# Attention and a gated MLP on one core: the attention of two batches as one stream of nine tiles

## The chip, the cores and the metric

The kernel runs on one core of one Trainium2 chip. The metric is the time of one execution on the device in microseconds; the time before is the median of three runs. The trace comes from a further, profiled execution. Engines are named as the profile names them: PE is TensorE (PEld its weight loads), DVE VectorE, ACT ScalarE, POOL GpSimd, SP SyncE, whose queue issues the transfers.

## The reference

Eight batches of 8 heads, 576 tokens and 64 elements a head go through attention in chunks of 64 tokens, then through an MLP whose gate mixes the tokens of a batch:

```python
scores = scale * np.matmul(q_c, k_c.transpose(0, 1, 2, 4, 3))      # per chunk of 64 tokens
attn = np.exp(scores - np.max(scores, axis=-1, keepdims=True))
attn = attn / (np.sum(attn, axis=-1, keepdims=True) + 1e-09)
x = heads_side_by_side(np.matmul(attn, v_c))                       # 8 x 576 x 512
h = gelu_tanh(x @ w_in)                                            # 512 -> 1024
u, v = (h[..., :512], h[..., 512:])
v_n = (v - mean(v)) / np.sqrt(var(v) + 1e-06) * g_ln
v_s = np.einsum('ts,bsd->btd', w_sg, v_n) + b_sg[None, :, None]    # over the 576 tokens
return x + (u * v_s) @ w_out
```

The inputs are spread so that one float32 rounding does not do: the kernel splits each operand of a large product into a high and a low part and adds three products.

## The kernel before

**Tiles of attention.** The 8 x 576 tokens are 36 tiles of 128 tokens, counted through all batches. 576 is four and a half tiles, so the tiles that begin in a batch of even number are five (the fifth lies half in the next batch), in one of odd number four: batch 2 has tiles 9 to 13, batch 3 tiles 14 to 17. `last` and `first` (lines 257 and 258) hold the bounds. From tile 5 on, a tile goes through three steps. S, the scores (`att_scores`, L315: 16 matmuls on 64x64 quadrants, 32 records in the trace, into a half of the tile `banks`), with the softmax behind it: maximum (L324), addition (L338) and sum (L342) on DVE, the exponential on ACT (L341), the scaling by the reciprocal sum on POOL (L345). T, the transposition (`att_transpose`: DVE in blocks of 32 at L359, ACT and DVE copies into `ptT` at L362 to L369). O, the outputs (`att_out`, L397: 16 small matmuls a tile, a pair of tiles into one accumulator `pm`), and `keep`, which copies them out as `xf`, as high part `xh` (ACT, L93) and low part `xl` (DVE, L96). S and O take one tile or a pair.

**Units of the MLP.** A batch has v units (12 matmuls of 128x512, L439; five in an even batch, of which the last, m = 4, takes the first 64 tokens of this batch and of the next from `xodd`; four in an odd one), four u units (L476), four s units (the mixing of tokens, 28 matmuls of 128x288, L496) and four o units (24, L519). I write v0 to v4, u0 to u3, s0 to s3, o0 to o3. Behind v and u stands a Gelu on ACT (L442, L483), and behind v the normalisation: DVE (L445 to L447), a power on POOL (L448), high part on ACT (L456) and low part on DVE (L457). Behind s the product with u on DVE (`gt`, L500), its high part on ACT (`gh`) and its low part on DVE (`gl`); every o unit needs `gh` and `gl` of all four s units, those of s3 in its last quarter. Behind o the residual addition on DVE (L527) and the store on SP. Exponential and Gelu stand in different tables of ACT; where one follows the other, the program has an ACT_TABLE_LOAD.

**Buffers.** Accumulators `pm` come from a ring of three in PSUM (`ps_m`, L89), for units and outputs alike. `xh`, `xl`, `gh` and `gl` of a batch share a ring of four places (tag `big`, L409, L410, L505, L506). The tiles q, k, v have four places (`QKV_BUFS`); `scores` issues the loads up to two tiles beyond its own (L540).

**Order.** The opening is written out in `START` (L45), up to the o units of batch 0 and the u units of batch 1. Then for every batch b from 1 on the units run in the order v, u, s, o, and `att_slots` (L543) hangs the steps of the next batch's attention behind units by their number: `"10:T0"` is the transposition of that batch's tile 0 behind unit 10. `SLOTS` (L56) has one list for a next batch of four tiles (b even, 17 units) and one for five (b odd, 16 units). Within this, a scheduler may still move instructions where their operands are expected to be ready. Each engine then works through its instructions in order.

Of the kernel before, what the change touches and what calls it, by code (L numbers as in the profile page):

```python
# [11 lines left out]
F32R = mybir.dt.float32r  # L12
# [9 lines left out]
B, H, S, D = 8, 8, 576, 64  # L22
P = 128
# [3 lines left out]
NT = B * S // P  # L27
HP = H // 2
KT = DM // P
# [14 lines left out]

START = """  # L45
L0 A0 A1 L1 S0 L2 T0 D11 A2 W0 A3 W1 L3 A4 S1 W2 S2 w0 w1 W3 T1 O0 w2 S3 O1 T2 w3 D14 A5 O2 T3 S4 O3 M0 X0 T4 X1 v00
O4 x0 v01 x1 X2 v02 X3 x2 v03 x3 v04 Y0 u00 u01 G0 Y1 u02 P5 u03 T5 s00 T6 s01 Q5 P7 Y2 s02 T7 Y3 s03 T8 v10 Q7 v11 Y4 v12 Y5 v13 u10 Y6 u11 Y7 u12 u13 o00 o01 o02 o03
"""

PE_TILES = 5  # L50
# [2 lines left out]

SLOTS = {  # L56
    4: "8:S01 10:T0 11:T1 12:O01 12:S23 14:T2 15:T3 16:O23",
    5: "7:S01 8:T0 9:T1 10:O01 10:S23 11:S4 12:T2 13:T3 14:T4 15:O23 15:O4",
}


# [6 lines left out]
def segments(t):  # L68

    out, at, end = [], t * P, (t + 1) * P  # L70
    while at < end:
        b = at // S
        stop = min(end, (b + 1) * S)
        out.append((b, at - t * P, at - b * S, stop - at))
        at = stop
    return out
# [3 lines left out]
def block_attention_gated_mlp(ctx: ExitStack, tc: tile.TileContext, qkv, w_in, w_out, w_sg, g_ln, b_sg, out):  # L80
# [3 lines left out]
    xp = ctx.enter_context(tc.tile_pool(name="xp", bufs=2))  # L84
# [6 lines left out]
    def split(hi, lo, src, hi_eng, lo_eng):  # L91
        if hi_eng is nc.scalar:
            nc.scalar.copy(hi, src)  # L93
        else:
            hi_eng.tensor_copy(hi, src)
        lo_eng.tensor_tensor(lo, src, hi.bitcast(F32), op=ALU.subtract)  # L96
# [160 lines left out]
    last = [((b + 1) * S - 1) // P for b in range(B)]  # L257
    first = [0] + [last[b] + 1 for b in range(B - 1)]
    xf, xh, xl, xodd = {}, {}, {}, {}
# [112 lines left out]
    def att_out(*tiles):  # L372
# [29 lines left out]
        for t, xo in zip(tiles, xos):  # L402
            keep(t, xo)

    def keep(t, xo):
        for b, at, off, n in segments(t):
            if b not in xf:
                xf[b] = xp.tile([P, HP, S], F32, name="xf")
                xh[b] = xp.tile([P, HP, S], F32R, name="xh", tag="big", bufs=4)  # L409
                xl[b] = xp.tile([P, HP, S], F32R, name="xl", tag="big", bufs=4)  # L410
            cs = slice(at // D, (at + n) // D)
            src = xo[:, cs]
            dst = [a[b][:, :, off : off + n].rearrange("p hp (c s) -> p c hp s", s=D) for a in (xh, xl, xf)]
            if f"l{t}" in ON_POOL:
                nc.scalar.copy(dst[2], src)
                split(dst[0], dst[1], dst[2], nc.scalar, nc.gpsimd)
            else:
                split(dst[0], dst[1], src, nc.scalar, nc.vector)
                nc.scalar.copy(dst[2], src)  # L419
            if off == 0:  # L420
                if b % 2 == 0:
                    xodd[0] = [xp.tile([P, HP, 2 * ODD], F32R, name=f"xodd_{i}", bufs=1) for i in range(2)]
                c = slice(b % 2 * ODD, (b % 2 + 1) * ODD)
                for dst, src in zip(xodd[0], (xh[b], xl[b])):
                    nc.scalar.copy(dst[:, :, c], src[:, :, 0:ODD].bitcast(F32))
# [59 lines left out]
    gh, gl = {}, {}  # L485

    def s_unit(b, dt):
        pm = ps_m.tile([P, 2, 512], F32, name="pm")
        dc = slice(dt * P, (dt + 1) * P)
        ops = []  # L490
        for m in range(4):
            ops += [(vl[m], wsg_h, m), (vh[m], wsg_l, m), (vh[m], wsg_h, m)]
        ops += [(z2[b % 2], wsg_l, 4), (z1[b % 2], wsg_h, 4)]
        for i, (a, c, m) in enumerate(ops):
            for j in range(2):
                nc.tensor.matmul(  # L496
                    pm[:, j, :HS], a[:, dc], c[:, m, j * HS : (j + 1) * HS], start=(i == 0), stop=(i == len(ops) - 1)
                )
        gt = tmp.tile([P, S], F32, name="gt", tag="tmp")
        nc.vector.tensor_tensor(  # L500
            gt.rearrange("p (a c) -> p a c", a=2), pm[:, :, :HS],
            u2[0][:, dt, :].rearrange("p (a c) -> p a c", a=2), op=ALU.mult,
        )
        if dt == 0:
            gh[b] = xp.tile([P, KT, S], F32R, name="gh", tag="big", bufs=4)  # L505
            gl[b] = xp.tile([P, KT, S], F32R, name="gl", tag="big", bufs=4)  # L506
        split(gh[b][:, dt, :S], gl[b][:, dt, :S], gt, nc.scalar, nc.vector)

    def o_unit(b, et):
# [33 lines left out]
    def att_slots(b, n):  # L543

        slots = [[] for _ in range(n)]
        for step in SLOTS[last[b] + 1 - first[b]].split():
            i, what = step.split(":")
            f = {"S": scores, "T": att_transpose, "O": att_out}[what[0]]
            slots[int(i)].append((f, [first[b] + int(k) for k in what[1:]]))
        return slots  # L550

    steps = {
# [3 lines left out]
    for name, f in zip("vuso", (v_unit, u_unit, s_unit, o_unit)):  # L556
        steps[name] = (lambda f: lambda k: f(k // 10, k % 10))(f)
# [12 lines left out]
    for b in range(1, B):  # L570
        units = [(v_unit, m) for m in range(4 if b % 2 else 5)]
        units += [(u_unit, i) for i in range(4)]
        units += [(s_unit, i) for i in range(4)] + [(o_unit, i) for i in range(4)]
        slots = att_slots(b + 1, len(units)) if b + 1 < B else [[]] * len(units)
        for i, ((f, k), after) in enumerate(zip(units, slots)):
            if b > 1 or f in (s_unit, o_unit):
                f(b, k)
            for g, tiles in after:
                g(*tiles)
# [44 lines left out]
```

## Time and profile before

| | |
|---|---|
| median of 3 runs | 532.47 us (530.79 to 532.74) |
| profiled execution | 531.17 us, span 529.4 us |
| PE matmuls / weight loads | 504.3 us (95%) / 465.8 us (88%) |
| DVE, ACT, POOL | 350.3 us (66%), 261.8 us (49%), 79.7 us (15%) |
| TensorE clock granted | 0.996 of full speed |
| data moved | 46.57 MB, 88 GB/s on average |

A row of a timeline gives the start in us, the time to the end of the last instruction of the group, engine, line, operation, output and inputs, sizes and number of records; brackets name idle time of the engine before it and who ended it. Matmuls overlap, so the distance from start to start is their price, not the duration shown.

### The profile page before, as it was taken

How to read it: one execution, taken by the hardware profiler on the slowest of the kernel's cores; microseconds unless marked ns; L12 is line 12 of the kernel's file. 1: busy time of each engine (PE TensorE's matmuls, PEld its weight loads, DVE VectorE, ACT ScalarE, POOL GpSimd, SP SyncE). 2: the span in 40 equal slices, each digit the busy share in tenths (PEclk: the TensorE clock that was granted, in tenths of full speed). 3: DMA queues.
4: the chain of work that ended last, by engine and by line, in shares of the span. 5: the costliest groups of instructions: out<-in, count | busy, mean ns of one | idle time of the engine just before them, and what ended most of it. 6: DMA issues, size and time to landing. Idle time of an engine off the chain costs nothing.

```text
span 529.4 us, 12456 instructions
## 1 busy us (share of the span) xinstructions
PE 504.3 (95%) x5274; PEld 465.8 (88%) x5278; DVE 350.3 (66%) x718; ACT 261.8 (49%) x482; POOL 79.7 (15%) x80
## 2 busy tenths in 40 slices
PE   5989996989999999999999999999999999999996
PEld 4677896779989799999989799998999799998996
DVE  7989677797587556766387555767378564767042
ACT  4697665654163753554353753544363653545210
POOL 0122221210102121012002121012012021012000
PEclk9999998999999999999999999999999999999999
DMA  8832524113441700352032700352033700020002
GB/s 336 286 117 61 164 68 121 42 41 110 140 122 68 202 1 1 106 165 61 2 109 80 198 5 1 83 173 75 2 79 106 199 7 1 3 90 0 1 1 89
DMA packets 49594, 46.57 MB, mean 88 GB/s; under 512 B 35202, under 2 KB 39554, under 8 KB 49540
## 3 DMA queue, kind: packets, MB, share of 16 engines
q1 hardware_dynamic: 49540, 45.80, 28.8%
q8 instruction: 41, 0.67, 0.5%
q14 instruction: 13, 0.11, 0.1%
HBM read 36.34 MB, written 9.44 MB: 86 GB/s over the span
## 4 chain that ended last, share of the span: by engine, by line
PE 75%; DVE 11%; ACT 6%; DMA 3%; POOL 2%; issue 1%; SPq 0%; DVEq 0%; POOLq 0%
PE pm L519 19%; PE pm L496 19%; PE pm L476 17%; PE pm L439 15%; PE pm L397 3%; PE banks L315 2%; DMA wsg<-w_in 1%; DMA qkv_t<-qkv 1%; DVE xl L96 1%; POOL pt L345 1%; DVE den L342 1%; DVE gt L500 1%; DMA st<-w_out 1%; DVE pt L338 1%; ACT xf L419 1%
## 5 line engine op out<-in xcount | busy, mean ns | idle before, releaser
L496 PE MATMUL pm<-wsg,v 128*128 128x288 f32 x768 | 108.7, 297 | 0.0
L496 PEld LDWEIGHTS pm<-wsg,v 128*128 128x128 f32 x768 | 104.0, 189 | 0.7
L519 PE MATMUL pm<-gh,wout 128*128 128x288 f32 x512 | 91.2, 297 | 0.0
L519 PEld LDWEIGHTS pm<-gh,wout 128*128 128x128 f32 x512 | 75.8, 189 | 0.4
L345 POOL TENSOR_TENSOR pt<-pt,den 128x512 f32<-128x512 f32 x32 | 35.1, 1104 | 239.6 <-DVE den L344 119.2
L448 POOL TENSOR_TENSOR sm<-sm,neg_half 128x1 f32<-128x1 f32 x36 | 35.1, 976 | 152.6 <-DVE sm L447 149.9
L519 PE MATMUL pm<-gl,wout 128*128 128x288 f32 x256 | 55.6, 296 | 0.0
L476 PE MATMUL pm<-xh,win_l 128*128 128x288 f32 x256 | 55.1, 297 | 0.0
L476 PE MATMUL pm<-xh,win_h 128*128 128x288 f32 x256 | 55.0, 296 | 0.0
L476 PE MATMUL pm<-xl,win_h 128*128 128x288 f32 x256 | 55.0, 296 | 0.0
L439 PE MATMUL pm<-win_h,xl 128*128 128x512 f32 x128 | 51.9, 406 | 2.4 <-DVE xl L96 2.4
L439 PE MATMUL pm<-win_l,xh 128*128 128x512 f32 x128 | 51.0, 399 | 0.0
L439 PE MATMUL pm<-win_h,xh 128*128 128x512 f32 x128 | 50.7, 396 | 0.0
L324 DVE TENSOR_REDUCE nmax<-banks 128x8 f32<-128x512 f32 x31 | 21.2, 684 | 39.7 <-PE banks L315 39.6
L93 ACT CAST gh<-gt 128x576 fp32r<-128x576 f32 x32 | 21.6, 674 | 44.6 <-DVE gt L500 44.2
L476 PEld LDWEIGHTS pm<-xh,win_l 128*128 128x128 f32 x256 | 41.4, 188 | 0.8
L519 PEld LDWEIGHTS pm<-gl,wout 128*128 128x128 f32 x256 | 41.4, 189 | 0.0
L476 PEld LDWEIGHTS pm<-xh,win_h 128*128 128x128 f32 x256 | 41.1, 188 | 0.0
L476 PEld LDWEIGHTS pm<-xl,win_h 128*128 128x128 f32 x256 | 41.0, 189 | 0.0
L362 ACT COPY ptT<-blocks 128x512 f32<-128x512 f32 x31 | 19.2, 621 | 43.1 <-DVE blocks L359 31.3
L500 DVE TENSOR_TENSOR gt<-pm,u 128x576 f32<-128x576 f32 x32 | 24.1, 752 | 24.0 <-PE pm L496 23.8
L341 ACT ACTIVATE pt<-pt 128x512 f32<-128x512 f32 x34 | 21.5, 632 | 36.5 <-DVE pt L338 26.6
(125 smaller groups left out, 842.5 us busy)
## 6 DMA issues: line engine op xcount, KB each, us to landing
qkv_t<-qkv SPq DMA_DIRECT2D x32, 512.0 KB, 4.6
out_dram<-ot SPq DMA_DIRECT2D x31, 288.0 KB, 2.2
qkv_t<-qkv SPq DMA_DIRECT2D x124, 64.0 KB, 3.8
qkv_t<-qkv SPq DMA_DIRECT2D x3, 768.0 KB, 10.0
wsg<-w_in SPq DMA_DIRECT2D x4, 512.0 KB, 4.5
wout<-w_in SPq DMA_DIRECT2D x4, 512.0 KB, 8.1
st<-w_out SPq DMA_DIRECT2D x8, 256.0 KB, 2.7
stage<-w_sg SPq DMA_DIRECT2D x5, 288.0 KB, 2.8
```

Source lines behind the costliest of these rows:

```text
L93: nc.scalar.copy(hi, src)
L324: nc.vector.tensor_reduce(nmax if t < PE_TILES else nmax.rearrange("p (c hp) -> p c hp", c=2), sc, axis=AX.X, op=ALU.max, negate=True)
L341: nc.scalar.activation(pt, pt, AF.Exp, scale=scale)
L345: (nc.gpsimd if t > last[1] else pick(f"n{t}")).tensor_tensor(pt, pt, den.unsqueeze(2).broadcast_to([P, H, D]), op=ALU.mult)
L362: nc.scalar.copy(ptT, blocks)
L397: nc.tensor.matmul(xo[o, c, h // 2, :], qt[r, 2, place, :], ptT[r, place].rearrange("p a s -> p (a s)"), start=True, stop=True,)
L439: nc.tensor.matmul(pv, a[:, kt, tok], c[:, kt, DH:], start=(i == 0), stop=(i == 11))
L448: nc.gpsimd.tensor_tensor(rs, rs, neg_half, op=ALU.pow)
L476: nc.tensor.matmul(pm[:, j, :HS], a[:, kt, dc], c[:, kt, j * HS : (j + 1) * HS], start=(i == 0), stop=(i == 11))
L496: nc.tensor.matmul(pm[:, j, :HS], a[:, dc], c[:, m, j * HS : (j + 1) * HS], start=(i == 0), stop=(i == len(ops) - 1))
L500: nc.vector.tensor_tensor(gt.rearrange("p (a c) -> p a c", a=2), pm[:, :, :HS], u2[0][:, dt, :].rearrange("p (a c) -> p a c", a=2), op=ALU ...
L519: nc.tensor.matmul(pm[:, j, :HS], a[:, kt, ec], c[:, kt, j * HS : (j + 1) * HS], start=(i == 0), stop=(i == len(ops) - 1),)
```

## The change

Two batches are treated as one stream of nine tiles. The list for an odd b now counts its tiles from those of batch b + 1, the list for an even b goes on with tile 4 of the same nine, which lie from `first[b]`. Steps that no longer exist (beyond tile 35) are left out. Outputs of a pair and the scores of the next pair stand behind the same unit. `START` gets `P9` (scores of tiles 9 and 10) between `o01` and `o02`, and `T9 T10` at its end; a list "first" serves batch 1. The four shared buffers become two by two, by the parity of the batch.

```diff
 SLOTS = {
-    4: "8:S01 10:T0 11:T1 12:O01 12:S23 14:T2 15:T3 16:O23",
-    5: "7:S01 8:T0 9:T1 10:O01 10:S23 11:S4 12:T2 13:T3 14:T4 15:O23 15:O4",
+    "first": "8:O01 8:S23 10:T2 11:T3 11:O23 11:S4 13:T4",
+    1: "0:T0 1:T1 5:O01 5:S23 8:T2 9:T3 10:O23 10:S4 13:T4",
+    0: "0:O4 0:S56 5:T5 6:T6 8:O56 8:S78 11:T7 12:T8 14:O78 14:S9A",
 }
...
-                xh[b] = xp.tile([P, HP, S], F32R, name="xh", tag="big", bufs=4)
-                xl[b] = xp.tile([P, HP, S], F32R, name="xl", tag="big", bufs=4)
+                xh[b] = xp.tile([P, HP, S], F32R, name="xh", tag=f"big_{b % 2}")
+                xl[b] = xp.tile([P, HP, S], F32R, name="xl", tag=f"big_{b % 2}")
...
-            gh[b] = xp.tile([P, KT, S], F32R, name="gh", tag="big", bufs=4)
-            gl[b] = xp.tile([P, KT, S], F32R, name="gl", tag="big", bufs=4)
+            gh[b] = xp.tile([P, KT, S], F32R, name="gh", tag=f"big_{b % 2}")
+            gl[b] = xp.tile([P, KT, S], F32R, name="gl", tag=f"big_{b % 2}")
...
-        for step in SLOTS[last[b] + 1 - first[b]].split():
+        for step in SLOTS["first" if b == 1 else b % 2].split() if b + 1 < B else ():
             i, what = step.split(":")
             f = {"S": scores, "T": att_transpose, "O": att_out}[what[0]]
-            slots[int(i)].append((f, [first[b] + int(k) for k in what[1:]]))
+            tiles = [first[b + b % 2] + int(k, 16) for k in what[1:]]
+            if tiles[0] < NT:
+                slots[int(i)].append((f, tiles))
...
-        slots = att_slots(b + 1, len(units)) if b + 1 < B else [[]] * len(units)
+        slots = att_slots(b, len(units))
```

(The pool `xp` has two buffers a tag where nothing is said, so `big_0` and `big_1` have two places each. Lines behind `SLOTS` stand two lower in the changed kernel: L397 becomes L399, L315 L317, L439 L441, L496 L498, L519 L521.)

Where it shows in the program's order: first PE in batch 3, from the block behind s2 to the start of o0; L397 is the outputs, L315 the scores, L496 an s unit, L519 an o unit. Before:

```order
L397 MATMUL pm<-ptT,qkv_t 64x64 x32
L315 MATMUL banks<-qkv_t 64x64 x32
L496 MATMUL pm<-wsg_754,v 128x288 x2
...
L519 MATMUL pm<-gh,wout_687 128x288 x2
L519 MATMUL pm<-gl,wout_686 128x288 x2
L315 MATMUL banks<-qkv_t 64x64 x16
L519 MATMUL pm<-gh,wout_686 128x288 x2
```

The same place in the changed kernel:

```order
L399 MATMUL pm<-ptT,qkv_t 64x64 x32
L317 MATMUL banks<-qkv_t 64x64 x16
L498 MATMUL pm<-wsg_754,v 128x288 x2
...
L521 MATMUL pm<-gh,wout_687 128x288 x2
L521 MATMUL pm<-gl,wout_686 128x288 x2
L521 MATMUL pm<-gh,wout_686 128x288 x2
```

The block behind s2 now ends with the scores of the fifth tile, and no small matmul stands between s3 and the o units.

Then PE where batch 3 ends and batch 4 begins (L439 is a v unit). Before:

```order
L519 MATMUL pm<-gh,wout_686 128x288 x2
L397 MATMUL pm<-ptT,qkv_t 64x64 x32
L315 MATMUL banks<-qkv_t 64x64
L397 MATMUL pm<-ptT,qkv_t 64x64
L439 MATMUL pm<-win_h,xl 128x512
L397 MATMUL pm<-ptT,qkv_t 64x64 x15
L439 MATMUL pm<-win_l,xh 128x512
...
L315 MATMUL banks<-qkv_t 64x64 x7
```

The same place in the changed kernel:

```order
L521 MATMUL pm<-gh,wout_686 128x288 x2
L441 MATMUL pm<-win_h,xl 128x512
L441 MATMUL pm<-win_l,xh 128x512
L441 MATMUL pm<-win_h,xh 128x512
...
L399 MATMUL pm<-ptT,qkv_t 64x64 x16
L317 MATMUL banks<-qkv_t 64x64 x32
```

The pair's outputs have gone to earlier units; the fifth tile's outputs stand in one piece behind v0, with the scores of the next pair.

Last ACT in the v stage of batch 4, where the Gelu is L442 (L444) and the exponential of the softmax L341 (L343). Before:

```order
L425 CAST xodd_3302<-xl 128x4x64
L442 ACT_TABLE_LOAD
L442 ACTIVATE hs<-pm 128x512 x2
L456 ACTIVATE v<-hs,sm 128x512
L442 ACTIVATE hs<-pm 128x512
```

The same place in the changed kernel:

```order
L427 CAST xodd_3149<-xl 128x4x64
L444 ACTIVATE hs<-pm 128x512
L343 ACT_TABLE_LOAD
L343 ACTIVATE pt<-pt 128x512 x2
L444 ACT_TABLE_LOAD
```

A pair of exponentials, with a table load on either side, now stands between two Gelus of the v stage.

## Rows read from the trace of the kernel before

**Rows 1.** Page, busy time of PE: us, share of the span, instructions.
```profile
PE 504.3 (95%) x5274; PEld 465.8 (88%) x5278; DVE 350.3 (66%) x718; ACT 261.8 (49%) x482; POOL 79.7 (15%) x80
```
**Rows 2.** Waits of PE: line, waited for, total us, times, longest.
```profile
PE pm L397 <- ACT ptT L367: 6.3, 6, 2.8
PE banks L315 <- DVE pt L338: 3.5, 3, 1.2
```
**Rows 3.** Chain of work, start and us: two batches apart, and the last batch.
```profile
218.34 0.93 PE banks L315 x64
...
338.43 0.93 PE banks L315 x64
...
484.92 12.80 PE pm L476 x96
497.72 14.91 PE pm L496 x112
512.64 12.79 PE pm L519 x96
```
**Rows 4.** Timeline of PE, batch 2: a block of outputs and scores.
```profile
216.55 0.69 PE L496 MATMUL pm<-wsg,z 128*128 128x288 f32 x4
...
219.20 0.54 PE L519 MATMUL pm<-gh,wout 128*128 128x288 f32 x2
219.58 0.42 PE L519 MATMUL pm<-gl,wout 128*128 128x288 f32 x2
```
**Rows 5.** Timeline of PE, end of batch 6: a block of outputs alone.
```profile
472.00 0.43 PE L519 MATMUL pm<-gh,wout 128*128 128x288 f32 x2
472.36 1.16 PE L397 MATMUL pm<-ptT,qkv_t 64*64 64x64 f32 x64
...
473.79 0.40 PE L439 MATMUL pm<-win_l,xh 128*128 128x512 f32 x1
474.02 0.40 PE L439 MATMUL pm<-win_h,xh 128*128 128x512 f32 x1
```
**Rows 6.** Chain of work, batch 3: a block of scores alone.
```profile
257.55 1.09 PE banks L315 x64
```
**Rows 7.** Timeline of PE, batch 3, behind s3 and at its end.
```profile
276.07 0.43 PE L519 MATMUL pm<-gl,wout 128*128 128x288 f32 x2
277.68 0.69 PE L315 MATMUL banks<-qkv_t 64*64 64x64 f32 x32 [1.18 <-DVE pt L338]
...
278.93 0.43 PE L519 MATMUL pm<-gl,wout 128*128 128x288 f32 x2
...
290.43 0.42 PE L519 MATMUL pm<-gh,wout 128*128 128x288 f32 x2
...
292.65 0.33 PE L397 MATMUL pm<-ptT,qkv_t 64*64 64x64 f32 x2 [0.61 <-ACT ptT L367]
...
297.45 0.40 PE L439 MATMUL pm<-win_l,xh 128*128 128x512 f32 x1
```
**Rows 8.** Page, costliest groups: maximum and exponential; busy us, mean ns.
```profile
L324 DVE TENSOR_REDUCE nmax<-banks 128x8 f32<-128x512 f32 x31 | 21.2, 684 | 39.7 <-PE banks L315 39.6
L341 ACT ACTIVATE pt<-pt 128x512 f32<-128x512 f32 x34 | 21.5, 632 | 36.5 <-DVE pt L338 26.6
```
**Rows 9.** Timeline of ACT, start of batch 2: a table load and its Gelu.
```profile
177.45 1.28 ACT L442 ACT_TABLE_LOAD   x1
178.74 0.60 ACT L442 ACTIVATE hs<-pm 128x512 f32<-128x512 f32 x1
```
**Rows 10.** Timeline of DVE, the product of s3 in batches 3 and 7.
```profile
277.62 0.75 DVE L500 TENSOR_TENSOR gt<-pm,u 128x576 f32<-128x576 f32 x1
...
512.67 0.76 DVE L500 TENSOR_TENSOR gt<-pm,u 128x576 f32<-128x576 f32 x1 [1.48 <-PE pm L496]
514.17 0.76 DVE L96 TENSOR_TENSOR gl<-gt,gh 128x576 fp32r<-128x576 f32 x1 [0.74 <-ACT gh L93]
```
**Rows 11.** Timeline of PE, batch 7: the first pair of o0.
```profile
512.48 0.43 PE L519 MATMUL pm<-gh,wout 128*128 128x288 f32 x2
```

More of the change, by code (lines that the diff above doesn't have):

```diff
@@ L46 @@
 L0 A0 A1 L1 S0 L2 T0 D11 A2 W0 A3 W1 L3 A4 S1 W2 S2 w0 w1 W3 T1 O0 w2 S3 O1 T2 w3 D14 A5 O2 T3 S4 O3 M0 X0 T4 X1 v00
-O4 x0 v01 x1 X2 v02 X3 x2 v03 x3 v04 Y0 u00 u01 G0 Y1 u02 P5 u03 T5 s00 T6 s01 Q5 P7 Y2 s02 T7 Y3 s03 T8 v10 Q7 v11 Y4 v12 Y5 v13 u10 Y6 u11 Y7 u12 u13 o00 o01 o02 o03
+O4 x0 v01 x1 X2 v02 X3 x2 v03 x3 v04 Y0 u00 u01 G0 Y1 u02 P5 u03 T5 s00 T6 s01 Q5 P7 Y2 s02 T7 Y3 s03 T8 v10 Q7 v11 Y4 v12 Y5 v13 u10 Y6 u11 Y7 u12 u13 o00 o01 P9 o02 o03 T9 T10
 """
```

## The prediction, before the changed kernel had run

> **What bounds the kernel now.** I read the busy times first: TensorE's matmuls cover 95% of the span [rows 1], so time comes back only where TensorE stands still or does something dearer than it must. Then the waits of TensorE by line, which show two that come back in several batches: the value product waits for ScalarE's copies of the transposed weights (6 waits, 6.3 us), and the scores wait for VectorE (3 waits, 3.5 us) [rows 2]. The three odd batches 1, 3 and 5 each have one wait of 1.18 for VectorE and one of 0.61 for ScalarE [rows 7]; 3 x 1.18 is all of the second line, and 3 x 0.61 leaves 4.5 us of the first to the opening, which the change leaves as it is.
>
> Then the chain, for what a stage costs when nothing stands in it: the last batch has no attention left and runs u in 12.80 us, s in 14.91, o in 12.79 [rows 3]. A v unit is 12 matmuls 0.23 apart [rows 5], 2.80. From one even batch's pair of scores to the same place two batches later is 338.43 - 218.34 = 120.09 us [rows 3]. Nine v units and two each of u, s and o make 25.2 + 81.0 = 106.2. So 13.9 us per two batches go to nine tiles of attention and to waiting for them. That is the only sum the change can touch.
>
> The timeline shows how these 13.9 are spent. I measure a block of 64x64 matmuls as the time it adds between the dense matmuls on both sides.
> - Outputs and scores of two pairs in one block: the last dense group begins at 216.55 and is due to end 0.53 later, at 217.08; the pair of matmuls after the block begins at 219.20, the next not 0.27 but 0.38 later. That makes 219.31 - 217.08 = 2.22 [rows 4].
> - Outputs alone: 473.79 - 0.23 - (472.00 + 0.27) = 1.29 [rows 5]. Scores of a pair alone take 1.09 in the chain [rows 6]; with about 0.1 of delay at either boundary, as in rows 4, I give them the same 1.29; where a fragment of them has run earlier and 48 records are left, I put 1.08, halfway to the 0.88 of 32 records, next.
> - In an odd batch the fifth tile's scores stand alone behind the first o matmuls: 276.07 + 0.27 to 278.93 - 0.53 is 2.06, of which 1.18 is waiting and 0.88 the block. At its end a pair of outputs, the fifth tile's outputs in two pieces around a matmul of v, and a part of the next scores: 290.43 + 0.27 to 297.45 - 0.23 is 6.52; less the v unit, 3.72, of which 0.61 is waiting and 3.11 blocks [rows 7].
>
> So an odd batch pays 1.29 + 2.22 + 0.88 + 3.11 = 7.50 and 1.79 of waiting, an even one 1.08 + 2.22 + 1.29 = 4.59. Together 13.88: the 13.9 are accounted for.
>
> **The change part by part.** No matmul is added or removed; the order moves. By the order of the changed kernel an even batch has three blocks and an odd one two, where there were three and six places: nine become five per two batches. Three of the five are two outputs with two scores, 2.22 each. Two have three tiles (96 records); I put these halfway between 1.29 and 2.22, 1.75.
> - Batches 2 and 3, and 4 and 5: 3 x 2.22 + 2 x 1.75 = 10.16 for 7.50 + 4.59 = 12.09. Gain 1.9 each, 3.8 together.
> - Batch 6, with no batch after its successor: 1.75 + 2.22 + 1.29 = 5.26 for 4.59. Loss 0.7.
> - Batch 1: before 2.22 + 0.88 + 3.11 = 6.21. Now 2.22, then one output and one score (64 records, 1.29), then the second output split by an o matmul; I give that 1.1, the 0.88 of a 32-record block and one more boundary of 0.2. Gain 1.6. The remainder of its first scores is in both kernels a fragment inside or behind o0, which I set equal.
>
> Blocks together: 4.7 us.
>
> The old waits go: three odd batches x 1.79 = 5.4 us. The fifth tile's scores now go into banks that VectorE read five units earlier, and its output stands three units (o2, o3, v0) behind its transposition. What is late next:
> - In batch 1 the second output of a pair is right behind its transposition again, as the one that waited 0.61 [rows 7], and the gated product of s3 (0.76 [rows 10]) stands ahead of that transposition on VectorE. I take 1.3. The outputs of its first pair follow four copies of transposed weights that ScalarE makes in a row; I take 0.3, from 0 to that 0.61.
> - In odd batches no block lies any more between s3 and o0. The last batch shows that this place has next to no slack: the product of s3 begins at 512.67, its low part begins at 514.17 and ends at 514.93 [rows 10], and o0, begun at 512.48 [rows 11], asks for it ten pairs of 0.27 later, at 515.15. In the changed order VectorE has, between the products of s2 and s3, both low parts of x, and the maximum, the addition and the sum of one softmax. From the end of s2: product and low part to 2.3, low part of x to 3.0, maximum to 3.6, addition to 4.3 (each about as long as the maximum, 0.68 [rows 8]). The exponential (0.63) needs a table load (1.28 [rows 9]) that ScalarE has not done before, since a Gelu ran after the previous exponentials. With the load hidden the sum ends at 5.6, and s3 at 1.65 + 3.73 = 5.4: the slack takes the difference. With the load wholly behind the addition it ends at 6.9, and the product of s3 is 1.5 late, of which the two matmuls of o1 that stand in between and the slack take half: 0.75. I take 0.45 for batches 3 and 5.
> - In even batches only a transposition stands between product and low part, and it fits into the 0.75 in which VectorE waits there for ScalarE anyway [rows 10]: nothing. If the cover failed it would be 0.7 a batch.
>
> New waits: 1.3 + 0.3 + 0.9 = 2.5. Waits net: -2.9 us.
>
> ScalarE also gets ten table loads more (18 become 28 in the order), since softmaxes now stand among the Gelus of v and u. In the even batches a load, two exponentials and a load stand between the Gelu of the second v unit and that of the third. ScalarE needs 0.60 + 1.28 + 1.26 + 1.28 + 0.60 = 5.0 for it [rows 8, 9], and I add 1.7 for the part of VectorE's two maxima and two additions (4 x 0.68) that ScalarE must wait out: 6.7 from the end of the second unit. Accumulators come in threes (the outputs take one), so TensorE needs that third one when u0 begins, three v units or 8.4 us after. Slack 1.7: nothing, as long as the load takes what the row says. In the odd batches the same sequence stands before the Gelu of u2; there s1 needs it, after two units of u and one of s, with more slack.
>
> The places by parity are the same four buffers. In the order before, batch and place had the same parity already; without own places the early outputs of the next even batch would have claimed the odd batch's. That edit is a condition of the rest and costs nothing. Loads of q, k, v are issued at the scores before theirs, at least three s units of TensorE work ahead. Queued between them on the queue of SyncE are the stores of the outputs; a load that waits for its buffer is freed by the block at that very place, so no store is held.
>
> Sum against the profiled execution (531.17, span 529.4): -4.7 - 2.9 = -7.6, I round to -7.4 for pieces set equal: 523.8. The median of the runs lies 1.3 above that execution, so 532.47 - 7.4 = 525.1.
>
> The Trainium skill speaks against this step: "ScalarE: Activation LUTs", What ACT_TABLE_LOAD costs, counts a drain of about 1.38 us beside the load for each switch of set, 2.66 in all; its section Table sets: the hidden batching unit advises to do all of one set before the next. By the page the ten loads would take about 26.6 us of ScalarE (an estimate from its figure). The row shows 1.28, and the Gelu behind the load begins at its end [rows 9], so the trace shows no drain after it.
>
> **The rivals.**
> 1. A switch costs ScalarE about two loads' time. Mechanism here: 6.7 + 2.6 = 9.3 against 8.4 in the even batches, 0.9 of waiting x 3, and the product of s3 1.28 later in batches 3 and 5. That returns 5.3: 530.4. For it: the loads stand in a row of dependent work. Against: rows 9.
> 2. Slower: o0 right behind s3. In every batch but the last VectorE is still in other work when s3 ends, as it was in batch 3, where the product started at 277.62 [rows 10], 1.8 after the end of s3, and the wait for the scores hid it. With one more operation of 0.68 ahead and the slack of 0.2 taken off, 2.3; six batches cost 13.8 in place of the 0.9 counted: 525.1 + 12.9 = 538.0. It makes the kernel slower than before from (7.4 + 0.9) / 6 = 1.4 a batch. Against: one softmax stands there now, not two, and none in the even batches.
> 3. Joining blocks saves nothing, since the price lies in the small matmuls and not in the change between the kinds: only the waits remain, 532.47 - 2.9 = 529.6. Against it: 1.29 + 1.29 is more than 2.22 [rows 4, 5].
> 4. The new waits do not arise: 522.6.
>
> **How the numbers follow.** Forecast 525.1 (own range 523.3 to 527.5): 0.63. Rival 1: 0.11; rival 2: 0.07; rival 3: 0.12; rival 4: 0.07. The range 522.4 to 530.6 leaves out rival 2 and edges of the others. The line for a measurable change is 0.5%, that is 529.8 and 535.1. Faster: 0.63 + 0.07, half of rival 3 and a quarter of rival 1: 0.79. Slower: most of rival 2, 0.06. The same: 0.15.
>
> **What would show it.** TensorE's waits of 1.18 for the scores and 0.61 for the fifth tile's outputs must be gone from batches 3 and 5; the same stretch of two batches should be about 117 us; blocks of 96 records should add about 1.75. In batch 1 the second output should wait about 1.3 us; in batches 3 and 5 the first o unit should wait below 0.8 us for a low part. No matmul of u should wait for a Gelu. I am wrong if one does, if the joined blocks add more than 2.4, or if the even batches show a wait behind s3.

## The result, and the profile after

The changed kernel takes 526.59 us (median of 8 runs beside 8 of the kernel before, 532.78): the ratio is 0.988, 95% interval 0.9849 to 0.991. One of its eight runs took 1175.88 us and is left out of the ratio (the median without it is 526.36). Timed again later beside another kernel it was 524.77 (ratio 0.9871, 0.9837 to 0.9904). The forecast was 525.1, range 522.4 to 530.6; of the 7.4 us that it took off, 6.2 came. The profiled execution takes 524.2 us, span 522.4.

Its opening up to the u units of batch 1, which the change leaves alone, is not equally long from run to run: in the profiles of this study the first u matmul of batch 1 begins between 109.8 and 115.8 us. So I compare one stretch in all kernels, from that matmul to the end of the last o unit: before 512.64 + 12.79 - 112.46 = 412.97 us, changed 505.83 + 12.79 - 111.75 = 406.87, a gain of 6.1. Two more profiles of the changed order (experiments 11 and 7) gave 407.00 and 407.01, so a difference of 0.3 can be read.

The page's busy line of the changed kernel, against [rows 1]:

```profile
PE 500.8 (96%) x5278; PEld 464.0 (89%) x5278; DVE 346.9 (66%) x718; ACT 272.3 (52%) x492; POOL 78.8 (15%) x80
```

ScalarE has ten instructions more, the table loads, and is busy 10.5 us longer. TensorE's waits (line, waited for, total us, times, longest), against [rows 2]:

```profile
PE pm L399 <- ACT ptT L369: 5.5, 4, 2.8
...
PE pm L521 <- DVE gl L98: 1.2, 2, 0.6
...
PE pm L521 <- ACT gh L95: 0.4, 2, 0.2
```

The wait for the scores is gone, two of the six for transposed weights too; new is a wait of two o units for the low and high part. The chain of the changed kernel (start, us, what), against [rows 3, 4, 6]:

```profile
111.75 12.80 PE pm L478 x96
...
174.68 0.62 PE pm L399 x32
175.30 0.93 PE banks L317 x64
...
187.63 12.80 PE pm L478 x96
200.42 1.09 PE pm L399 x64
201.52 0.93 PE banks L317 x64
...
225.05 0.93 PE banks L317 x64
...
305.34 12.80 PE pm L478 x96
...
342.85 0.93 PE banks L317 x64
...
422.91 12.80 PE pm L478 x96
...
478.12 12.80 PE pm L478 x96
...
505.83 12.79 PE pm L521 x96
```

Two batches take 342.85 - 225.05 = 117.80 us where they took 120.09; the prediction asked for about 117. The same u units in the chain before:

```profile
112.46 12.80 PE pm L476 x96
...
188.48 12.80 PE pm L476 x96
...
308.57 12.80 PE pm L476 x96
...
428.65 12.80 PE pm L476 x96
```

From u0 to u0 the 6.1 can be dealt out, and set against the prediction's own terms (the 1.75 of the next v stage belongs to the interval in which it stands):

| from u0 of batch | before | after | measured | predicted |
|---|---|---|---|---|
| 1 to 2 | 76.02 | 75.88 | -0.14 | -1.6 - 1.79 + 1.6 + 1.75 = -0.04 |
| 2 to 4 | 120.09 | 117.71 | -2.38 | 10.16 - 12.09 - 1.79 + 0.45 = -3.27 |
| 4 to 6 | 120.08 | 117.57 | -2.51 | -3.27 |
| 6 to 7 | 56.27 | 55.21 | -1.06 | 2.22 + 1.29 - 4.59 = -1.08 |

The ends agree to 0.1 (the first in part by luck, see below). The two middle rows are 0.8 to 0.9 short, and both hold one odd batch. TensorE's timeline in batch 1 and in odd batch 3, against [rows 7]:

```profile
141.67 1.42 PE L399 MATMUL pm<-ptT,qkv_t 64*64 64x64 f32 x61
...
142.94 1.14 PE L317 MATMUL banks<-qkv_t 64*64 64x64 f32 x63
...
155.41 0.69 PE L399 MATMUL pm<-ptT,qkv_t 64*64 64x64 f32 x32
155.93 0.65 PE L317 MATMUL banks<-qkv_t 64*64 64x64 f32 x32
...
158.19 0.30 PE L399 MATMUL pm<-ptT,qkv_t 64*64 64x64 f32 x2 [1.02 <-ACT ptT L369]
...
275.29 0.43 PE L521 MATMUL pm<-gh,wout 128*128 128x288 f32 x2
...
278.05 0.78 PE L521 MATMUL pm<-gh,wout 128*128 128x288 f32 x4 [0.20 <-ACT gh L95]
279.46 0.53 PE L521 MATMUL pm<-gl,wout 128*128 128x288 f32 x2 [0.63 <-DVE gl L98]
279.83 0.42 PE L521 MATMUL pm<-gh,wout 128*128 128x288 f32 x2
```

In batch 1 the second output waits 1.02 where I put 1.3. The first pair shows no wait by name, but its scores begin 1.27 after its outputs (142.94 - 141.67), where the pair of batch 3 needs 0.98 (269.90 to 270.88): 0.29 lost, where I put 0.3. Its weight loads stand still from 142.19 to 142.49, after the first tile's outputs, while ScalarE copies transposed weights until 142.42. In batch 3 twelve pairs of 0.267 lie between 275.29 and the pair at 279.83; unhindered that would begin at 278.49. So o0 loses 1.34 us in batch 3, and 1.35 in batch 5 (393.09 to 397.64), where I put 0.45. VectorE there (brackets: idle before, and who ended it), against [rows 10]:

```profile
273.49 0.69 DVE L340 TENSOR_TENSOR pt<-banks,nmax 128x512 f32<-128x512 f32 x1
274.10 0.68 DVE L98 TENSOR_TENSOR xl<-pm,xh 128x512 fp32r<-128x512 f32 x1
275.94 0.69 DVE L344 TENSOR_REDUCE den<-pt 128x8 f32<-128x512 f32 x1 [1.16 <-ACT pt L343]
276.55 0.75 DVE L502 TENSOR_TENSOR gt<-pm,u 128x576 f32<-128x576 f32 x1
...
278.03 1.38 DVE L98 TENSOR_TENSOR gl<-gt,gh 128x576 fp32r<-128x576 f32 x1 [0.43 <-ACT gh L95]
```

ScalarE in the same place, and then at the third v unit of batch 4, against [rows 9]:

```profile
272.89 0.59 ACT L421 COPY xf<-pm 128x512 f32<-128x512 f32 x1 [0.94 <-DVE xl L98]
273.37 0.59 ACT L95 CAST xh<-pm 128x512 fp32r<-128x512 f32 x1
273.98 1.28 ACT L343 ACT_TABLE_LOAD   x1
275.28 0.63 ACT L343 ACTIVATE pt<-pt 128x512 f32<-128x512 f32 x1
...
301.36 1.28 ACT L444 ACT_TABLE_LOAD   x1
302.65 0.60 ACT L444 ACTIVATE hs<-pm 128x512 f32<-128x512 f32 x1
```

And GpSimd:

```profile
277.75 1.04 POOL L347 TENSOR_TENSOR pt<-pt,den 128x512 f32<-128x512 f32 x1 [16.59 <-DVE den L346]
```

Read together: the load starts at 273.98, just before the addition ends at 274.18, because ScalarE's queue holds two high parts and a copy of x ahead of it, and that copy itself stood 0.94 for VectorE's low part of x. VectorE then stands still 1.16 us for the exponential; the sum comes at 275.94 and the product of s3 at 276.55, 1.27 after s3's end at 275.28. Then the low part takes 1.38 and not 0.76, while GpSimd scales the weights beside it.

### The profile page after: what moved, and what is told of

Same layout as the page of the kernel before. It is cut to its first block, busy times and chain, and to the rows that moved or that the text cites. A ratio compares the mean times of both kernels' runs of the same rounds, so it can differ in the third digit from the quotient of the medians.

```text
span 522.4 us, 12455 instructions
## 1 busy us (share of the span) xinstructions
PE 500.8 (96%) x5278; PEld 464.0 (89%) x5278; DVE 346.9 (66%) x718; ACT 272.3 (52%) x492; POOL 78.8 (15%) x80
## 4 chain that ended last, share of the span: by engine, by line
PE 75%; DVE 12%; ACT 6%; DMA 2%; POOL 2%; issue 1%; SPq 0%; DVEq 0%; POOLq 0%; ACTq 0%
PE pm L498 19%; PE pm L521 19%; PE pm L478 17%; PE pm L441 15%; PE pm L399 3%; PE banks L317 2%; DMA stage<-w_sg 2%; DVE gt L502 1%; DVE gl L98 1%; DMA qkv_t<-qkv 1%; DVE xl L98 1%; POOL pt L347 1%; DVE den L344 1%; ACT gh L95 1%; DVE nmax L326 1%
## 5 line engine op out<-in xcount | busy, mean ns | idle before, releaser
L498 PE MATMUL pm<-wsg,v 128*128 128x288 f32 x768 | 108.3, 297 | 0.0
L498 PEld LDWEIGHTS pm<-wsg,v 128*128 128x128 f32 x768 | 104.0, 189 | 0.5
L521 PE MATMUL pm<-gh,wout 128*128 128x288 f32 x512 | 92.3, 297 | 0.4 <-ACT gh L95 0.4
L521 PEld LDWEIGHTS pm<-gh,wout 128*128 128x128 f32 x512 | 76.0, 188 | 1.3 <-ACT gh L95 0.9
L521 PE MATMUL pm<-gl,wout 128*128 128x288 f32 x256 | 55.8, 296 | 1.2 <-DVE gl L98 1.2
L441 PE MATMUL pm<-win_h,xl 128*128 128x512 f32 x128 | 51.3, 401 | 1.8 <-DVE xl L98 1.8
L441 PE MATMUL pm<-win_l,xh 128*128 128x512 f32 x128 | 50.7, 396 | 0.0
L441 PE MATMUL pm<-win_h,xh 128*128 128x512 f32 x128 | 50.6, 396 | 0.0
L529 DVE TENSOR_TENSOR ot<-pm,xf 128x576 f32<-128x576 f32 (+1 forms) x33 | 24.2, 734 | 38.3 <-PE pm L521 38.3
L521 PEld LDWEIGHTS pm<-gl,wout 128*128 128x128 f32 x256 | 41.4, 189 | 1.8 <-DVE gl L98 1.7
L447 DVE BATCH_NORM_STATS2 sm<-hs 128x6 f32<-128x512 f32 x36 | 24.7, 687 | 23.3 <-ACT hs L444 23.1
L98 DVE TENSOR_TENSOR xl<-pm,xh 128x512 fp32r<-128x512 f32 (+1 forms) x34 | 21.7, 639 | 23.8 <-ACT xh L95 23.8
```

What stands on the lines that cost most here:

```text
L441: nc.tensor.matmul(pv, a[:, kt, tok], c[:, kt, DH:], start=(i == 0), stop=(i == 11))
L447: nc.vector.bn_stats(st, h)
L498: nc.tensor.matmul(pm[:, j, :HS], a[:, dc], c[:, m, j * HS : (j + 1) * HS], start=(i == 0), stop=(i == len(ops) - 1))
L521: nc.tensor.matmul(pm[:, j, :HS], a[:, kt, ec], c[:, kt, j * HS : (j + 1) * HS], start=(i == 0), stop=(i == len(ops) - 1),)
L529: nc.vector.tensor_tensor(ot[:, js], pm[:, js, :HS], res[:, js], op=ALU.add)
```

## The experiments

All are compared by the stretch. My theory after the result: blocks and old waits went as forecast; the missing 1.8 us are o0's wait in batches 3 and 5, from the unhidden table load and from GpSimd. Rival: it is VectorE's own work at that place, whatever the load does.

**1. The odd batches' block one unit later, behind s3.**

```diff
-    1: "0:T0 1:T1 5:O01 5:S23 8:T2 9:T3 10:O23 10:S4 13:T4",
+    1: "0:T0 1:T1 5:O01 5:S23 8:T2 9:T3 11:O23 11:S4 13:T4",
```

> In batches 3 and 5 the outputs of the second pair and the scores of the fifth tile stand behind s3 instead of behind s2. My theory: the changed kernel loses 1.34 us in each of these two batches in the first o unit (0.20 + 0.63 idle, the rest slow pieces) because the products of s3 come late and nothing covers them; with the block there the waits of 0.20 and 0.63 are gone and the stretch from the first u matmul of batch 1 to the last o matmul, 406.9 us in the changed kernel, becomes about 404.2. Rival: the block only moves the wait, since the low parts of x and the softmax then stand in front of the residual additions and the accumulators of o2 come late: 406.9 or more.

Measured 506.41 + 12.79 - 114.87 = 404.33, 2.54 less. No o unit waits. Nearly all of the 2.7 lost in these batches lies between s3 and o0.

**2. One table for all.** Exponentials in place of both Gelus, so that ScalarE never changes its table behind the opening.

```diff
-        nc.scalar.activation(h, pv, AF.Gelu_apprx_tanh)
+        nc.scalar.activation(h, pv, AF.Exp)
...
-        nc.scalar.activation(hs, pm[:, :, :HS], AF.Gelu_apprx_tanh)
+        nc.scalar.activation(hs, pm[:, :, :HS], AF.Exp)
```

> The changed kernel with the exponential in place of Gelu in all units, so that ScalarE never changes its table; the output is another. My theory: in batches 3 and 5 the sum of the fifth tile's softmax waits for a table load of 1.28 us, and that makes the product of s3 1.36 late. Without loads the product starts within 0.3 of the end of s3, the idle 0.83 per batch falls to 0.3 or less, and the stretch of 406.9 us becomes about 405. Rival A: VectorE's queue of two low parts and a softmax makes the product late with or without a load: waits stay at 0.8, stretch within 0.3 of 406.9. Rival B: loads also hold up the Gelus of v and u and with them TensorE: the stretch falls below 404.

Measured 408.34: a miss. The waits of o0 did go (the sum began before s3's end, and the low part took 0.76). But three new waits came in the even batches, of u3 for the Gelu's replacement behind u0, 2.5 us together: the scheduler put the work of ScalarE and VectorE in another order, presumably since its estimates now held no loads. So the sum says nothing of the loads' price. Why the new order costs just that I did not settle.

**3. The same edit on the kernel before.**

> The kernel before with the exponential in place of Gelu; the output is another. It gives what loads cost there. My theory: nothing on TensorE's path, since each load stands at a change of stage; the stretch of 413.0 us stays within 0.4, the waits of 1.18 and 0.61 stay. If loads cost in the order before as well, it falls by more.

Measured 413.09 for 412.97, and the waits of 1.18 stay: without loads the kernel before is not faster. Here too the scheduler moved some work of ScalarE and VectorE, so this is weaker evidence that loads cost it nothing.

**4. Scaling of the fifth tile on VectorE.**

```diff
-        (nc.gpsimd if t > last[1] else pick(f"n{t}")).tensor_tensor(
+        (nc.gpsimd if t > last[1] and t not in (22, 31) else pick(f"n{t}")).tensor_tensor(
```

> The scaling of the softmax of tiles 22 and 31 (the fifth tiles of batches 4 and 6) goes from GpSimd to VectorE. In the changed kernel the low part of s3 in batches 3 and 5 lasts 1.38 us instead of 0.76 while GpSimd scales (1.04 us). My theory: the two engines exclude each other in these two-input operations; with the scaling elsewhere the low part lasts 0.76 again. It ends 0.3 earlier if VectorE does the scaling in the time in which it waits for ScalarE, and up to 0.4 later if the scaling (about 0.7) stands in front of it wholly. Rival: the low part is slow because ScalarE writes its high part or since the operands lie as they do: it still lasts about 1.38.

Measured 405.75, 1.12 less, although VectorE now has 0.69 more to do ahead of the low part. Its timeline:

```profile
280.69 0.69 DVE L347 TENSOR_TENSOR pt<-pt,den 128x512 f32<-128x512 f32 x1
281.30 0.75 DVE L98 TENSOR_TENSOR gl<-gt,gh 128x576 fp32r<-128x576 f32 x1
```

The low part takes 0.75 again. With the scaling away from GpSimd an odd batch gains 0.56.

**5. The load earlier.** A tiny exponential behind the second transposition lets ScalarE load the table in time in which it was idle.

```diff
+            if t in (21, 30):
+                warm = small.tile([P, H], F32, name="nmax")
+                nc.scalar.activation(warm[D : D + 32, 0:1], ptT[D : D + 32, 0, 1, 0:1], AF.Exp)
         state[t] = (qt, ptT)
```

> The changed kernel with one exponential of 32 elements, read from the last copy of the transposed weights and used by nothing, behind the second transposition of batches 3 and 5, so that ScalarE loads the table of the exponential before s2 ends and not behind the addition of the softmax. (VectorE's two small operations on the sum come ahead of the product of s3 in this order, about 0.4 us.) Theory: the load of 1.28 behind the addition is what makes the sum, and so the product of s3, late: the sum of the fifth tile starts at or before the end of s3 (0.75 after it in the changed kernel), the low part ends about 1.1 us earlier, o0's waits shrink from 1.34 to 0.1 to 0.4 in each of the two batches, stretch 404.6 to 405.1 for 406.87. Rival: VectorE's own work is what makes the product late and the load lies beside it: sum and product start where they did, stretch 406.9 or, with the small operations ahead, 407.5.

Measured 507.91 + 12.79 - 115.70 = 405.00, 1.87 less, and no o unit waits by name. It is the clean form of experiment 2: VectorE's timeline shows the sum right behind its neighbours, with no idle time ahead, 0.4 before s3's end at 279.25:

```profile
278.06 0.68 DVE L98 TENSOR_TENSOR xl<-pm,xh 128x512 fp32r<-128x512 f32 x1
278.84 0.69 DVE L344 TENSOR_REDUCE den<-pt 128x8 f32<-128x512 f32 x1
...
281.33 0.76 DVE L98 TENSOR_TENSOR gl<-gt,gh 128x576 fp32r<-128x576 f32 x1 [0.74 <-ACT gh L95]
```

TensorE's, at the same place:

```profile
279.25 0.43 PE L524 MATMUL pm<-gh,wout 128*128 128x288 f32 x2
...
282.51 0.70 PE L524 MATMUL pm<-gh,wout 128*128 128x288 f32 x4
```

The pair at 282.51 is due eleven pairs after 279.25, at 282.19: o0 loses 0.32 where it lost 1.34. The rival falls as the main cause: VectorE's work is the same, and three quarters of batch 3's loss are gone. Here GpSimd's scaling ends at 281.17, before the low part starts, so this gain and the last overlap and are not to be added.

**6. Joined blocks split again**, five of them, by one unit each; four transpositions go one unit later with them.

```diff
-    1: "0:T0 1:T1 5:O01 5:S23 8:T2 9:T3 10:O23 10:S4 13:T4",
+    1: "1:T0 2:T1 5:O01 5:S23 8:T2 9:T3 10:O23 10:S4 13:T4",
-    0: "0:O4 0:S56 5:T5 6:T6 8:O56 8:S78 11:T7 12:T8 14:O78 14:S9A",
+    0: "0:O4 0:S56 5:T5 6:T6 8:O56 9:S78 12:T7 13:T8 14:O78 15:S9A",
```

> The changed kernel with five of its joined blocks split by one unit of dense work each (in the list for odd batches also two transpositions one unit later). Theory: a joined block of 2 outputs and 2 scores adds 2.22, the same apart 1.29 + 1.29 = 2.58; so each split costs about 0.36 and the stretch grows by 5 x 0.36 = 1.8 at the least bound of two even batches with two splits each and one more: 408.0 to 408.9, with no new wait of TensorE. Rival (joining saves nothing): 406.9 within 0.4.

Measured 408.78: 1.91 for five, 0.38 each, with no new wait. Joining saves what the prediction took, and rival 3 falls.

**7. One ring of four places again.**

```diff
-                xh[b] = xp.tile([P, HP, S], F32R, name="xh", tag=f"big_{b % 2}")
+                xh[b] = xp.tile([P, HP, S], F32R, name="xh", tag="big", bufs=4)
```

(`xl`, `gh` and `gl` likewise.)

> The changed order with one ring of four places for xh, xl, gh and gl again, as before the change. Stretch from the first u matmul of batch 1 to the end of the last o: 406.87 us in the changed kernel. Theory (the places by parity are a condition of the rest, worth nothing by themselves): the outputs of the first pair of an even batch, which stand behind s0's neighbourhood of the odd batch before it, now ask for places that this odd batch's xh and xl hold until its last u matmul; the block's copies wait, the accumulator comes free later, and TensorE waits about 2.5 to 4 us in batches 3 and 5: stretch 412 to 415. Rival: the copies come behind the last u unit anyway, nothing waits, 406.9 within 0.4.

Measured 407.01: nothing, against my theory. The instructions stand in the same order, and ScalarE's copy of the early outputs waits 0.47 for their matmuls and for nothing else, as in the changed kernel. The new order does not need places of its own here; the trace does not show which places the copies took.

**8. The kernel before with the fifth tile's scores a unit later**, so that the 1.18 has nothing to wait for.

```diff
-    5: "7:S01 8:T0 9:T1 10:O01 10:S23 11:S4 12:T2 13:T3 14:T4 15:O23 15:O4",
+    5: "7:S01 8:T0 9:T1 10:O01 10:S23 12:S4 12:T2 13:T3 14:T4 15:O23 15:O4",
```

> The kernel before, with the scores of the fifth tile one unit later (behind o0 in place of inside it), so that the three waits of 1.18 for the scores have nothing to wait for. Stretch in the kernel before: 412.97. Theory: the 1.18 hid the late product of s3, which starts 1.8 after the end of s3 because of VectorE's work for the softmaxes; with the wait gone o0 waits for its low part in its place, and the stretch falls by less than 1 us in all: 412.0 to 413.0, with a wait of the o unit for gl of 0.8 to 1.2 in batches 1, 3 and 5. Rival: the waits go and nothing comes: 412.97 - 3 x 1.18 = 409.4.

Measured 519.42 + 12.79 - 115.75 = 416.46, 3.5 more than before. Both expectations miss, the rival by far more. TensorE's timeline in batch 3:

```profile
283.08 0.53 PE L519 MATMUL pm<-gh,wout 128*128 128x288 f32 x2 [0.75 <-DMA qkv_t<-qkv]
283.54 0.33 PE L315 MATMUL banks<-qkv_t 64*64 64x64 f32 x2
284.28 0.53 PE L519 MATMUL pm<-gl,wout 128*128 128x288 f32 x2 [0.42 <-DVE gl L96]
284.65 0.42 PE L519 MATMUL pm<-gh,wout 128*128 128x288 f32 x2
285.01 0.91 PE L315 MATMUL banks<-qkv_t 64*64 64x64 f32 x30
```

The late product takes the old wait's place (0.75 and 0.42; in batches 1 and 5 the 0.75 is put down to the high part, here to a transfer), and the scores now break into o0 twice. From s0's start to the next outputs, batches 1 and 5 lose 0.68 each. Batch 3 loses 2.16; its extra stands in a stretch at a lower clock (last section). 3 x 0.68 + 1.5 is the 3.5. A wait removed by itself was a loss: what the change gained from the 1.18 came from moving the scores before s3, together with the outputs.

**9 to 11. Both late places moved.** Experiment 1, and batch 1's last block one unit later too.

```diff
-    "first": "8:O01 8:S23 10:T2 11:T3 11:O23 11:S4 13:T4",
+    "first": "8:O01 8:S23 10:T2 11:T3 12:O23 12:S4 14:T4",
```

> The odd batches' block behind s3 (as in the run with that alone, 404.33) and batch 1's last block one unit later too, so that the second output of its pair is further behind its transposition and no longer split from the scores. Theory: the wait of 1.02 in batch 1 goes, and one boundary (about 0.36) with it: stretch 402.7 to 403.3. Rival: the o unit of batch 1 then waits for the low part of s3 in its place, as batches 3 and 5 did: 404.0 to 404.7.

Measured 504.12 + 12.79 - 114.44 = 402.47, 1.86 less than experiment 1: the wait of 1.02, and 0.84 for a block that is no longer split. By the stretch it beats both kernels, and it was timed with the changed kernel beside it:

> The same kernel as the run with both blocks one unit later, timed: by its stretch (402.47 for 412.97 before and 406.87 changed) 10.5 us less than before, 522 us, ratio 0.980; a rival that the other stretches pay for it: above 524, ratio above 0.984.

> The changed kernel again, on the same chip as the timed run beside it: by the stretch 6.1 us less than before, ratio 0.988, and 4.4 us more than with both blocks later.

522.06 us, ratio to before 0.981 (0.978 to 0.984), stretch 402.48; the changed kernel 524.77, ratio 0.9871 (0.9837 to 0.9904), stretch 407.00. The medians differ by 2.7, less than the stretch's 4.5; the lowest times (520.19, 524.13) differ by 3.9, and the two profiled ones, both at a mean granted clock of 0.989, by 4.9 (522.00, 526.92). The chain in batch 3 of the faster order has the block behind s3 and a dense o stage behind it:

```profile
274.03 1.09 PE pm L399 x64
275.12 0.47 PE banks L317 x32
275.58 12.99 PE pm L521 x96
```

## Why the prediction was right, and where not

Right, step by step:
- **Where time can come from.** 13.9 us per two batches for attention, its blocks priced by what they add between dense matmuls: the last row of the table agrees to 0.1 us, and splitting costs 0.38 a block, where 1.29 + 1.29 - 2.22 is 0.36. Rival 3 put it at nothing. The 96-record block in the v stage of batch 4 adds 1.75, as put: the matmuls of v around it begin at 292.00 and 294.21, which leaves 294.21 - 0.23 - (292.00 + 0.23) = 1.75.
- **The old waits.** 1.18 and 0.61 are gone from batches 3 and 5.
- **Even batches.** In batch 4 the third v unit's Gelu starts at the end of the load and ends at 303.25, u0's first matmul begins at 305.18: slack 1.9 where I worked out 1.7, and no u matmul waits. Rival 1 needed 2.6 more.
- **Rival 2** is the mechanism that acts in batches 3 and 5, but with 1.34 in two batches, not 2.3 in six. Rival 4 falls with it: the new waits do arise.

The step that failed is a term's size: "I take 0.45 for batches 3 and 5". It was 1.34, and two things made it so. I put the price of the late product between the load hidden and "the load wholly behind the addition", and took about the middle. It was nearly wholly behind: I had counted VectorE's operations there one by one, but not ScalarE's queue, in which the high parts of x and a copy stand ahead of the load; the sum ended 6.8 after the end of s2, against my outer end of 6.9. For that end the prediction itself has 0.75. And I gave the low part its 0.76 although GpSimd's scaling falls beside it: it took 0.62 more (experiment 4), a term I had at nothing, though in the trace of the kernel before six low parts lasted 0.94 or 1.17. 0.75 + 0.62 is 1.37, close to the 1.34. Moving the load takes the loss to 0.32, but moves the low part away from the scaling as well, so what the load alone costs is not measured.

Luck lies in the first row of the table. Its wait was 0.28 shorter than put, and its split block 0.2 dearer than the 1.1 put: experiment 9 gained 0.84 by joining it, where 1.29 + 1.1 - 1.75 is 0.64. The two nearly cancel. With 1.34 in place of 0.45, 1.02 in place of 1.3 and 1.3 in place of 1.1 the sum of 7.6 becomes 7.6 - 1.8 + 0.3 - 0.2 = 5.9, against 6.1 measured. The 0.2 that I took off in rounding to 7.4 had no row behind it.

A second statement failed at no cost to the time: that places by parity are "a condition of the rest" (experiment 7).

## What to carry to other kernels

Price a block of small matmuls by what it adds between the dense ones on both sides, and join blocks: each boundary saved was worth 0.2 us here, wherever no engine was late. When a wait is moved away, work out what every engine's queue (not only the slow one's) holds ahead of the next operand TensorE asks for; here ScalarE's queue and a GpSimd neighbour tripled a small term. Where the last product before a dependent stage is late, a block of independent matmuls in front of that stage can cover it (experiment 1); the same matmuls inside the stage did not (experiment 8).

## What the hardware showed

**VectorE waits for GpSimd on operands in SBUF.** The low part (both inputs in SBUF) takes 0.76 alone and 1.38 beside GpSimd's scaling: it ends at 279.41, 0.62 after GpSimd's 278.79. In the kernel before the same operation took 0.94 (265.55, ending 0.62 after GpSimd's end at 265.87) in batch 3 and 1.17 in batch 2, again ending 0.62 after GpSimd's operation. The Trainium skill, "SBUF — State Buffer", Who interferes with whom, states that the pair of ports shared by the two is an exclusive lock. The constant 0.62 behind GpSimd's end, whatever the overlap, agrees with a lock and not with a shared bandwidth.

**The clock falls in places.** Rows of the stretches of three profiles (from:to, length, PE, PEld, DVE, ACT, POOL busy, granted clock, DMA share, GB/s): the opening of the changed kernel in its first and its last profile, and experiment 8 behind o0's waits.

```profile
78.00:92.00 14.00, 10.00 (x171) 9.24 (x171) 11.00 (x22) 7.33 (x14) 1.38 (x1) 0.88 0.41 115
```

```profile
78.00:92.00 14.00, 9.96 (x163) 9.20 (x162) 10.71 (x21) 7.33 (x14) 1.38 (x1) 0.76 0.43 115
```

```profile
285.00:289.00 4.00, 4.00 (x45) 3.88 (x45) 3.27 (x7) 2.05 (x4) 0.73 (x1) 0.57 0.19 74
```

The same instructions got 0.88 in one profile and 0.76 in another, in a stretch in which TensorE is busy 10 of 14 us; both are mixtures of the two levels, 1.2 and 2.4 GHz. The 24 matmuls of an s unit that begin at 87.50 in both take 3.57 us in the one and 4.61 in the other, 1.0 of the 2.6 by which these two openings differ. In experiment 8 batch 3 ran mostly at the lower level (0.57 of 2.4 GHz is near 1.2 GHz) for 4 us after TensorE had been busy only 3.82 of the 5 us before, while batches 1 and 5, with the same instructions and waits, stayed at full clock. What decides between them these runs do not show.
